# Moving one turn, three row loads, four bit copies and two late products in a fused hash-attention and SwiGLU kernel

## The chip, the core and the metric

The kernel runs on one core of a Trainium2 chip. A core has five engines with a queue each: TensorE (PE, matrix products; its weight loads are shown as PEld), VectorE (DVE), ScalarE (ACT), GpSimd (POOL) and SyncE (SP, which here only starts DMAs). Each engine takes its instructions strictly in the order of its queue; an instruction that waits holds up all behind it. The metric is device time of one execution in microseconds (us), the smaller the better.

## The reference

Attention in which a query sees only the keys of its own hash bucket, and then a gated feed-forward layer on the result:

```python
q_bits = (einsum('bhsd,dk->bhsk', q, proj) > 0)      # 6 bits for each token
k_bits = (einsum('bhsd,dk->bhsk', k, proj) > 0)
mask   = q_bucket[..., :, None] == k_bucket[..., None, :]
scores = where(mask, q @ k.T / sqrt(64), -1e9)
attn   = softmax(scores)                             # denominator + 1e-9
x      = (attn @ v), heads side by side              # 3072 x 512
xn     = x / sqrt(mean(x*x) + 1e-6) * rms_g
out    = (silu(xn @ w_gate) * (xn @ w_val)) @ w_out
```

q, k and v are (4, 8, 768, 64) in float32, proj is 64 x 6, w_gate and w_val are 512 x 1536, w_out is 1536 x 512; out is 3072 x 512 in float32.

## The kernel before

**Tiles.** The mask costs no product of its own: beside the 64 rows of a head, the operands of the score product (the tiles QK, six buffers that rotate) carry 12 rows of hash bits, scaled so that a pair of tokens of different buckets gets a score that exp takes to nothing. So the contraction runs over 76 rows (`KROWS`), or over 128 where the buffer's rows 64 to 127 were cleared with zeros once (`clear_rows`, line 138; `score_rows`, line 141).

Work goes by half units: a pair of key tiles of one head, for one half `w` of a batch (384 tokens, eight halves in all). `SLOTS` lists them, 6 for each pair of heads, in the order of `TURNS`: half 0 with head pair 0, half 1 with pair 0, half 0 with pairs 1, 2 and 3, half 1 with pairs 1, 2, 3, then batch 1 likewise. Pair 2 of half 0 is half units 18 to 23. In each half unit PE makes the scores (`scores`, lines 350 to 358, into s_ps, two buffers), ACT the exponentials (`probs`, line 365, into psb), and some half units later PE the product with v (`av`, line 377, into o_ps, of which there is one buffer). After two heads DVE takes o_ps out (`attn_out`, otmp of line 392, rcp of line 397); then x is otmp times rcp and sq is x squared (`attn_x`, lines 404 and 416, on POOL, or on DVE for pairs 2 and 3 of half 0), and DVE sums sq over the columns (`sumsq`, line 420). When all four pairs of a half are summed, the norm (lines 427 to 433), the scaling and the turning of x follow, and the feed-forward layer of that half is spread over the half units that come after (lines 473 to 503).

**Inputs.** Rows of q, k and v come by DMA from SP's queue into nine raw buffers (`load_rows`, line 113; 384 KB for a pair of heads). A new load waits until the old content of its buffer has been used. PE turns the rows (`turn_pe`, t_ps of line 181), DVE copies the result to kT and qT (`keep`, line 189), POOL and some ACT copies cast it into QK (`cast_half`, lines 195 and 197). The hash is a product of kT, qT and proj on PE (line 221, d_ps) and a comparison on DVE (`signs`, line 228); the bits are then copied into the rows of QK by DVE (lines 261 and 281) or by small DMAs on SP (lines 259 and 279). For pair 2 the hash is made at half unit 12; its first four bit blocks are copied by DVE, the other four by SP, and scores 19 are the first to need one of SP's.

**The order.** It is written out by hand: `at(s, f, ...)` puts a step into half unit `s` of `plan`, with a rank, and the loop at the end issues for each half unit the scores of the next one, the steps of rank below 3, the exponentials, and then the other steps by rank:

```python
for s in range(NS + 48):
    if 1 < s + 1 < NS:
        scores(s + 1)
    todo = steps(s)
    n = sum(r < 3 for r, _, _ in todo) if s < NS - 1 else 0
    for _, _, f in todo[:n]:
        f()
    if s < NS - 1:
        probs(s + 1)
    for _, _, f in todo[n:]:
        f()
```

What one half unit issues on an engine stands behind all that earlier ones issued there. The weights of the feed-forward layer (wg, wv, wo) are loaded by DMAs that POOL starts (lines 549 and 555); a load in POOL's queue stands behind the casts and products issued before it.

`idle` (line 345) makes products of ones with ones whose result nobody reads; eight stand ahead of scores 0 and six ahead of scores 3.

Of the kernel before, what the change touches and what calls it, by code (L numbers as in the profile page):

```python
# [8 lines left out]
FP32 = mybir.dt.float32  # L9
# [7 lines left out]
S = 768  # L17
# [31 lines left out]
def kernel(  # L49
# [34 lines left out]
    pq = const.tile([128, 48], FP32, name="pq")  # L84
    thr = const.tile([128, 1], FP32, name="thr")
    scl = const.tile([128, 1], FP32, name="scl")
    mhalf = const.tile([128, 3], FP32, name="mhalf")
# [49 lines left out]

    def clear_rows(i):
        nc.gpsimd.memset(qkbuf[i][D:128].rearrange("p h n -> p (h n)").bitcast(FP32), 0.0)

    def score_rows(b, hp):
        return slice(0, 128 if (b, hp) in ((1, 0), (1, 1)) or b > 1 else KROWS)

# [206 lines left out]
    def scores(g):  # L350
        w, h, p = SLOTS[g]
        ps = scps.tile([128, 2, 512], FP32, name="s_ps")
        idle(ps[:, 0, HALF:512], {0: 8, 3: 6}.get(g, 0))
        for j in range(2):
            nc.tensor.matmul(  # L355
                ps[:, j, 0:HALF], k_cols(w // 2, h, 2 * p + j), q_cols(w, h),
                start=True, stop=True,
            )
        sps[g] = ps
# [25 lines left out]
    def attn_out(w, hp):  # L385
        b = w // 2
        if w not in x:
            x[w] = xpool.tile([128, 3, DMODEL], FP32, name="x")
            ssp[w] = xpool.tile([128, 3, 4], FP32, name="ssp")
        o = ot.pop((w, hp))  # L390
        tmp = spool.tile([128, 3, 2, 66], FP32, name="otmp")
        nc.vector.tensor_add(  # L392
            tmp[:, :, :, 0:65], o[:, :, :, 0:65],
            cvb[b % 2][:, 2 * hp : 2 * hp + 2, 0:65].unsqueeze(1).to_broadcast([128, 3, 2, 65]),
        )
        r = spool.tile([128, 3, 2, 1], FP32, name="rcp")
        nc.vector.reciprocal(r, tmp[:, :, :, 64:65])  # L397
        return tmp, r

    def attn_x(w, hp, tmp, r):  # L400
        xd = x[w][:, :, 128 * hp : 128 * hp + 128]
        urgent = (w, hp) in ((0, 2), (0, 3))
        eng = nc.vector if urgent else nc.gpsimd
        eng.tensor_mul(  # L404
            xd.rearrange("p c (h d) -> p c h d", h=2), tmp[:, :, :, 0:64],
            r.to_broadcast([128, 3, 2, 64]),
        )
        sq = spool.tile([128, 3, 128], FP32, name="sq")
        if urgent:
            for c in range(3):  # L410
                nc.vector.scalar_tensor_tensor(
                    out=sq[:, c], in0=xd[:, c], scalar=1.0, in1=xd[:, c],
                    op0=ALU.mult, op1=ALU.mult, accum_out=ssp[w][:, c, hp : hp + 1],
                )
        else:
            nc.gpsimd.tensor_mul(sq, xd, xd)  # L416
        return sq
# [98 lines left out]

    nc.vector.memset(ones16, 1.0)
    make_identity(nc, ident)
    nc.gpsimd.dma_start(out=pn[64:128], in_=proj)
# [22 lines left out]
    for i in range(2):  # L542
        nc.gpsimd.memset(vls[i][:, :, :, 64:65], 1.0)
        nc.gpsimd.memset(vsum[i][:, :, 64:65], 6.0)
    clear_rows(4)
    clear_rows(5)

# [36 lines left out]
    cast_half(0, 0, "q", 0, nc.scalar)  # L584
    columns_of_proj()
    idle(wz[:, 0:128], 5)
    bits0 = hash_head(0)
# [37 lines left out]
    for h in range(2):  # L625
        at(1 + h, cast_half, 0, h, "q", 1)
        at(h, (bits0, bits1)[h], (nc.vector,), 3)

    for hp, turns, sv in ((1, (1, 2, 3, 5), 8), (2, (7, 8, 9, 10), 17), (3, (12, 13, 14, 15), 22)):
        for i, s in enumerate(turns):  # L630
            at(s, keep_pair, 0, hp, i)
            at(s + 1, casts, 0, hp, i)
            if i % 2:
                at(s + 2, cast_half, 0, 2 * hp + i // 2, "q", 0, nc.scalar)
        at(sv, v_prep, 0, hp)

    for h, s in ((2, 4), (3, 7)):
        at(s, hash_one, h)
        for t in range(3):
            at(s + 1 + t, lambda h=h, t=t: moves[h]((nc.vector,), t), rank=5)  # L640
    for hp, s, slots in ((2, 12, (13, 14, 15, 16)), (3, 17, (18, 19, 20, 21))):
        at(s, hash_pair, 0, hp)
# [4 lines left out]
    for i, (t, src) in enumerate(((wg, moe_w_gate), (wv, moe_w_val))):  # L647
        at(2 + 4 * i, load_w, t, src, 0, 768)
        at(19 + 5 * i, load_w, t, src, 768, 1536)
        at(38 + 7 * i, load_wo, 6 * i, 6 * i + 6)  # L650
# [4 lines left out]
    for hp, loads, turns, sh, evens, sv in (  # L655
        (0, (9, 11, 13), (20, 21, 24, 27), 33, (41, 42), (27, 44)),
        (1, (13, 14, 36), (29, 31, 33, 35), 40, (45, 47), (49, 51)),
    ):
# [42 lines left out]

    for i, s in ((2, 76), (3, 78), (0, 97), (1, 98)):
        at(s, clear_rows, i, rank=6)
# [22 lines left out]
    for w in range(8):  # L726
        for h in range(H):
# [85 lines left out]
```

## Time and profile before

| what | value |
|---|---|
| median of three runs | 329.41 us (329.21 to 329.52) |
| the profiled execution | 329.47 us |
| its span on the core | 327.6 us |
| PE busy | 321.5 us, 98% |
| DVE, ACT, POOL busy | 72%, 64%, 50% |
| granted PE clock | 0.998 |

In the rows of a timeline the first number is the start in us from the span's start, the second the time until the end of the last of the merged instructions; then come engine, line, operation, output and input, their shapes, and how many instructions are merged. In brackets stands the idle time of the engine just before, and what ended it. A row of windows gives the stretch, its length, the busy time of PE, PEld, DVE, ACT and POOL with the number of instructions, the granted clock, the DMA engines' mean share, and GB/s. In a row of the chain stand start, length, and what the time went to.

### The profile page before, as it was taken

To read this page: it belongs to the slowest core of one execution; us is meant where nothing else is said; L and a number is where in the kernel's file an instruction comes from. 1 tells how busy PE (TensorE), PEld (TensorE's weight loads), DVE (VectorE), ACT (ScalarE), POOL (GpSimd) and SP (SyncE) were. 2 spreads that over 40 slices of the span, in tenths; PEclk is the share of its full clock that TensorE was granted. 3 is DMA by queue.
4 is the path that set the end of the run, shared out by engine and by line. 5 is a ranking of instruction groups with operands and counts; after the bars stand their busy time and mean duration, and the time that the engine had idled before them with its cause. 6 is when DMAs were issued, how large, how long until landed. Compare 5 with 4: busy or idle time off the path is not lost.

```text
span 327.6 us, 7853 instructions
## 1 busy us (share of the span) xinstructions
PE 321.5 (98%) x2975; PEld 199.5 (61%) x2975; DVE 234.9 (72%) x526; ACT 208.1 (64%) x324; POOL 165.4 (50%) x238
## 2 busy tenths in 40 slices
PE   8998999999999999999999999999999999999995
PEld 7576766655566556655566656566566656655654
DVE  4798896888598976989487865967267824793860
ACT  3788986775576666657576766667677766423331
POOL 7887977278658685686734274733221320230000
PEclk9999999999999999999999999999999999999999
DMA  7998988984359729911470814001200012002002
GB/s 216 358 212 244 165 131 154 151 179 70 119 109 172 128 48 226 155 39 26 130 128 18 150 24 152 3 18 22 78 32 2 11 24 98 0 3 96 2 0 97
DMA packets 85509, 32.69 MB, mean 100 GB/s; under 512 B 70376, under 2 KB 82400, under 8 KB 85472
## 3 DMA queue, kind: packets, MB, share of 16 engines
q1 hardware_dynamic: 81392, 27.28, 35.2%
q0 software_dynamic: 3712, 4.72, 9.3%
q8 instruction: 23, 0.38, 0.5%
q10 hardware_dynamic: 368, 0.20, 0.2%
q14 instruction: 14, 0.11, 0.1%
HBM read 28.58 MB, written 6.29 MB: 106 GB/s over the span
## 4 chain that ended last, share of the span: by engine, by line
PE 94%; DMA 2%; ACT 2%; DVE 0%; issue 0%; DVEq 0%; ACTq 0%
PE v_ps L483 19%; PE s_ps L355 19%; PE y_ps L496 18%; PE g_ps L473 15%; PE o_ps L377 10%; PE d_ps L221 4%; PE s_ps L473 4%; PE t_ps L181 2%; DMA QK<-bits 2%; ACT psb L365 1%; PE z_ps L348 1%; PE x_ps L458 1%; DMA out_dram<-ysb 1%; PE m_ps L336 1%; DVE bits L228 0%
## 5 line engine op out<-in xcount | busy, mean ns | idle before, releaser
L365 ACT ACTIVATE psb<-s_ps 128x768 f16<-128x768 f32 x192 | 150.7, 809 | 30.1 <-PE s_ps L355 28.1
L355 PE MATMUL s_ps<-QK 128*128 128x384 f16 (+1 forms) x384 | 93.7, 326 | 1.3 <-DMA QK<-bits 0.5
L483 PE MATMUL v_ps<-xnT,wv 128*128 128x384 f16 x384 | 78.1, 326 | 0.0
L496 PE MATMUL y_ps<-wo,ht 128*128 128x512 f16 x276 | 69.2, 379 | 0.0
L404 POOL TENSOR_TENSOR x<-otmp,rcp 128x384 f32<-128x384 f32 x30 | 25.7, 857 | 83.4 <-DVE rcp L397 83.2
L377 PEld LDWEIGHTS <-psb 128*128 128x128 f16 x1152 | 51.7, 98 | 21.8 <-issue 3.7
L475 ACT ACTIVATE t<-g_ps 128x384 f32<-128x384 f32 x78 | 38.2, 490 | 40.7 <-PE g_ps L473 38.2
L473 PE MATMUL g_ps<-xnT,wg 128*128 128x384 f16 x312 | 63.5, 326 | 0.0
L484 DVE SCALAR_TENSOR_TENSOR t<-t,g_ps 128x384 f32<-128x384 f32 x78 | 42.9, 550 | 28.3 <-ACT t L475 28.2
L485 DVE SCALAR_TENSOR_TENSOR ht<-t,v_ps 128x384 f16<-128x384 f32 x96 | 53.2, 554 | 11.5 <-PE v_ps L483 1.0
L377 PE MATMUL o_ps<-vl,psb 128*128 128x65 f16 x1152 | 56.0, 193 | 0.0
L483 PEld LDWEIGHTS <-wv 128*128 128x128 f16 x384 | 36.5, 98 | 22.9
L473 PEld LDWEIGHTS <-wg 128*128 128x128 f16 x384 | 36.1, 98 | 23.0
L496 PEld LDWEIGHTS <-ht 128*128 128x128 f16 x276 | 26.3, 98 | 26.5 <-issue 2.1
L355 PEld LDWEIGHTS <-QK 128*128 128x128 f16 (+1 forms) x384 | 31.1, 97 | 16.8 <-issue 3.1
L503 ACT COPY ysb<-y_ps 128x512 f32<-128x512 f32 x23 | 13.5, 585 | 24.3 <-PE y_ps L496 23.7
L392 DVE TENSOR_TENSOR otmp<-o_ps,cvb 128x390 f32<-128x390 f32 x32 | 17.9, 559 | 14.9 <-PE o_ps L377 14.8
L416 POOL TENSOR_TENSOR sq<-x 128x384 f32<-128x384 f32 x30 | 25.5, 849 | 2.4
L213 POOL CAST QK<-kT 64x768 f16<-64x768 f32 x20 | 17.0, 848 | 10.8 <-DVE kT L205 8.9
L213 POOL CAST QK<-qT 64x768 f16<-64x768 f32 x20 | 16.5, 823 | 10.8 <-DVE qT L205 8.1
L205 DVE STREAM_TRANSPOSE kT<-kL 128x192 f32<-128x192 f32 x40 | 19.7, 521 | 0.0
L205 DVE STREAM_TRANSPOSE qT<-qL 128x192 f32<-128x192 f32 x40 | 19.4, 518 | 0.0
(81 smaller groups left out, 307.2 us busy)
## 6 DMA issues: line engine op xcount, KB each, us to landing
vL<-in_v_dram SPq DMA_DIRECT2D x16, 384.0 KB
out_dram<-ysb SPq DMA_DIRECT2D x23, 256.0 KB
kL<-in_k_dram SPq DMA_DIRECT2D x40, 96.0 KB
qL<-in_q_dram SPq DMA_DIRECT2D x40, 96.0 KB
kL<-in_k_dram SPq DMA_DIRECT2D x5, 384.0 KB
qL<-in_q_dram SPq DMA_DIRECT2D x5, 384.0 KB
wg<-in_moe_w_gate_dram POOLq DMA_DIRECT2D x2, 768.0 KB, 8.5
wv<-in_moe_w_val_dram POOLq DMA_DIRECT2D x2, 768.0 KB, 9.6
```

The costliest lines, as they stand in the source:

```text
L205: nc.vector.transpose(dst.rearrange("p (c t r) -> p r c t", c=6, r=4)[:, r : r + 1], src.rearrange("p (r c) d -> p r c d", r=4)[:, r : r + 1],
L213: nc.gpsimd.tensor_copy(QK[b, hp][0:64, hh, o : o + S], T0[b, hp, which][64 * hh : 64 * hh + 64, :])
L355: nc.tensor.matmul(ps[:, j, 0:HALF], k_cols(w // 2, h, 2 * p + j), q_cols(w, h), start=True, stop=True,)
L365: nc.scalar.activation(psb[w, h][:, p], sps.pop(g)[:, :, 0:HALF], AF.Exp, scale=ESCALE,)
L377: nc.tensor.matmul(o[:, c, hh, 0:65], psb[w, h][:, jt // 2, jt % 2, 128 * c : 128 * c + 128], vls[b % 2][:, h, v_chunk(b, h, jt), 0:65], s ...
L404: eng.tensor_mul(xd.rearrange("p c (h d) -> p c h d", h=2), tmp[:, :, :, 0:64], r.to_broadcast([128, 3, 2, 64]),)
L473: nc.tensor.matmul(g, wg[:, kt, fs], xnT[w][:, kt], start=(kt == 0), stop=(kt == 3))
L475: nc.scalar.activation(t, g, AF.Tanh, scale=0.5)
L483: nc.tensor.matmul(vv, wv[:, kt, fs], xnT[w][:, kt], start=(kt == 0), stop=(kt == 3))
L484: nc.vector.scalar_tensor_tensor(out=t, in0=t, scalar=1.0, in1=g, op0=ALU.add, op1=ALU.mult)
L485: nc.vector.scalar_tensor_tensor(out=ht[w][:, ft], in0=t, scalar=0.5, in1=vv, op0=ALU.mult, op1=ALU.mult)
L496: nc.tensor.matmul(y, ht[w][:, ft, c * 128 : (c + 1) * 128], wo[:, ft, :], start=(ft == 0), stop=(ft == NF - 1),)
```

## The change

- Scores 3 lose their six idle products. In the same place of PE's order stands the turn of q of head 2 (pair 1), which was one half unit later.
- The copies of the last bit block of heads 0 and 1 on DVE move from half units 0 and 1 to 2 and 4, to the end of each.
- The second bit copy of pair 2 on DVE moves from half unit 14 to 13.
- x and sq of pair 0 move to half units 22 (half 0; was 8) and 24 (half 1; was 17), and their sums to 24 and 26, ahead of the otmp of pair 2. The sum of pair 1 of half 0 moves from 24 to 22. otmp and rcp get a third buffer, sq has one instead of two.
- The row loads of batch 1 for pair 0 (k, q, v) move from half units 9, 11 and 13 to 3, 3 and 9, those of pair 1 (k, q) from 13 and 14 to 9. In SP's queue k and q of pair 0 now stand ahead of the bits of heads 2 and 3, and v, k, q ahead of those of pair 2.
- The second half of wg is loaded at half unit 21 instead of 19, that of wv at 25 instead of 24.
- Buffers 1, 2, 4 and 5 are cleared at the start, by POOL, POOL, ACT and DVE (in two parts), where it was 4 and 5 by POOL; buffer 0 follows at half unit 50 and 3 at 78, where it was 2, 3, 0 and 1 at 76 to 98. All scores but those of pairs 0 and 3 of batch 0 contract over 128 rows.

On POOL this gives the following order around half units 17 to 26, as the two kernels list it: v of pair 2; x, sq of pair 1; wg; two casts of kT; v of pair 3; a cast of qT; x, sq of pair 0 for half 0; x, sq of pair 0 for half 1; wv. On DVE the three sums stand one behind another, but for one copy of kT, just ahead of the otmp of pair 2.

```diff
-    def clear_rows(i):
-        nc.gpsimd.memset(qkbuf[i][D:128].rearrange("p h n -> p (h n)").bitcast(FP32), 0.0)
+    def clear_rows(i, eng=nc.gpsimd, heads=(0, 1)):
+        for h in (heads if eng is nc.vector else (0,)):
+            part = qkbuf[i][D:128, h] if eng is nc.vector else (
+                qkbuf[i][D:128].rearrange("p h n -> p (h n)"))
+            part = part.bitcast(FP32)
+            if eng is nc.scalar:
+                eng.copy(part, zcol[D:128].to_broadcast([D, 2 * S]))
+            else:
+                eng.memset(part, 0.0)
 
     def score_rows(b, hp):
-        return slice(0, 128 if (b, hp) in ((1, 0), (1, 1)) or b > 1 else KROWS)
+        return slice(0, KROWS if (b, hp) in ((0, 0), (0, 3)) else 128)
...
-        idle(ps[:, 0, HALF:512], {0: 8, 3: 6}.get(g, 0))
+        idle(ps[:, 0, HALF:512], {0: 8}.get(g, 0))
...
-        tmp = spool.tile([128, 3, 2, 66], FP32, name="otmp")
+        tmp = spool.tile([128, 3, 2, 66], FP32, name="otmp", bufs=3)
...
-        r = spool.tile([128, 3, 2, 1], FP32, name="rcp")
+        r = spool.tile([128, 3, 2, 1], FP32, name="rcp", bufs=3)
...
-        sq = spool.tile([128, 3, 128], FP32, name="sq")
+        sq = spool.tile([128, 3, 128], FP32, name="sq", bufs=1)
...
-    clear_rows(4)
-    clear_rows(5)
+    clear_rows(1)
+    clear_rows(2)
+    clear_rows(4, nc.scalar)
+    clear_rows(5, nc.vector, (0,))
...
     columns_of_proj()
+    clear_rows(5, nc.vector, (1,))
...
-        at(h, (bits0, bits1)[h], (nc.vector,), 3)
-
-    for hp, turns, sv in ((1, (1, 2, 3, 5), 8), (2, (7, 8, 9, 10), 17), (3, (12, 13, 14, 15), 22)):
+        at(2 + 2 * h, (bits0, bits1)[h], (nc.vector,), 3, rank=6)
+
+    for hp, turns, sv in ((1, (1, 1, 3, 5), 8), (2, (7, 8, 9, 10), 17), (3, (12, 13, 14, 15), 22)):
...
-    for hp, s, slots in ((2, 12, (13, 14, 15, 16)), (3, 17, (18, 19, 20, 21))):
+    for hp, s, slots in ((2, 12, (13, 13, 15, 16)), (3, 17, (18, 19, 20, 21))):
...
-        at(19 + 5 * i, load_w, t, src, 768, 1536)
+        at(21 + 4 * i, load_w, t, src, 768, 1536)
...
-        (0, (9, 11, 13), (20, 21, 24, 27), 33, (41, 42), (27, 44)),
-        (1, (13, 14, 36), (29, 31, 33, 35), 40, (45, 47), (49, 51)),
+        (0, (3, 3, 9), (20, 21, 24, 27), 33, (41, 42), (27, 44)),
+        (1, (9, 9, 36), (29, 31, 33, 35), 40, (45, 47), (49, 51)),
...
-    for i, s in ((2, 76), (3, 78), (0, 97), (1, 98)):
+    for i, s in ((0, 50), (3, 78)):
...
-                if (w, h) == (1, 1):
+                if w < 2 and h == 1:
                     at(end, o_first, w, 0, rank=4.5)
-                    at(end + 3, o_last, w, 0, rank=4.5)
+                    at(22 + 2 * w, o_last, w, 0, rank=4.5)
+                    at(24 + 2 * w, s_step, w, 0, rank=4)
                 else:
                     at(end, o_step, w, h // 2, rank=4.5)
-                if (w, h) not in ((0, 5), (0, 7)):
+                if (w, h) not in ((0, 1), (0, 5), (0, 7), (1, 1)):
                     late = 3 if h == 7 and w < 7 else 4
-                    at(end + late, s_step, w, h // 2, rank=5)
+                    if (w, h) == (0, 3):
+                        at(22, s_step, w, 1, rank=4)
+                    else:
+                        at(end + late, s_step, w, h // 2, rank=5)
```

More of the change, by code (lines that the diff above doesn't have):

```diff
@@ L85 @@
     thr = const.tile([128, 1], FP32, name="thr")
+    zcol = const.tile([128, 1], FP32, name="zcol")
     scl = const.tile([128, 1], FP32, name="scl")
@@ L517 @@
     nc.vector.memset(ones16, 1.0)
+    nc.vector.memset(zcol, 0.0)
     make_identity(nc, ident)
```

## The prediction

> **What bounds the kernel now.** I read the page first, then the windows, then the chain of waits, then each engine's timeline between 8 and 46 us.
>
> ```profile
> span 327.6 us, 7853 instructions
> PE 321.5 (98%) x2975; PEld 199.5 (61%) x2975; DVE 234.9 (72%) x526; ACT 208.1 (64%) x324; POOL 165.4 (50%) x238
> ...
> 20.00:30.00 10.00, 9.13 (x117) 6.03 (x116) 8.85 (x21) 8.51 (x15) 8.93 (x15) 1.00 0.93 228
> ...
> 50.00:60.00 10.00, 10.00 (x94) 6.46 (x92) 7.56 (x16) 7.72 (x14) 6.20 (x10) 1.00 0.91 152
> ...
> 22.78 0.68 DVE bits L228
> ...
> 23.48 5.21 DMA QK<-bits
> ...
> 28.83 0.34 PE s_ps L355
> ...
> 29.19 0.82 ACT psb L365
> ```
>
> PE is the bound. From 50 us its windows are full, so whatever time is won or lost ahead of that is carried to the end one for one. The loss lies in the attention-only start: 20 to 30 us lacks 0.87 us of PE, and the chain passes there from the hash bits of pair 2 through a DMA of 5.21 us to the scores. Every edit but the later clears falls in this start; I price each as a shift of PE at about 46 us, and carry it to the end.
>
> **The clears.** Two POOL clears stay where they were (other buffers). One more is a scalar copy of 1536 columns ahead of the first qT copy; DVE gets two of 768 columns, one ahead of its first kT copy, one ahead of the first signs.
>
> ```profile
> 5.54 0.48 ACT L189 COPY qT<-t_ps 128x384 f32<-128x384 f32 x1 [2.94 <-PE t_ps L181]
> ...
> 4.90 0.56 DVE L189 COPY kT<-t_ps 128x384 f32<-128x384 f32 x1 [1.40 <-PE t_ps L181]
> ...
> 6.98 0.68 DVE L228 TENSOR_SCALAR bits<-d_ps,thr,scl 128x384 f16<-128x384 f32 x1 [1.34 <-PE d_ps L221]
> ```
>
> Four copies of 384 columns are 1.92 us, inside ACT's idle 2.94. For a DVE clear the nearest row is a copy of 384 columns, 0.56, so 768 columns cost 1.12 at most, inside 1.40 and 1.34. These idle times are the cover; without it up to 1.1 us would stand ahead of the first hash, and below nothing it can't go, since nothing is taken away there. I take 0. The later clears are POOL's, three become one in the PE-full part: 0. Contraction over 128 rows instead of 76 leaves the product its 384 columns: 0.
>
> **The turn in the place of idle products, and two bit moves put back.**
>
> ```profile
> 10.97 0.50 PE L348 MATMUL s_ps<-ones 128*128 128x128 f16 x6 [0.24 <-ACT psb L365]
> 11.30 0.49 PE L355 MATMUL s_ps<-QK 76*128 76x384 f16 x2
> ...
> 10.54 0.50 POOL L261 COPY QK<-bits 12x384 f16<-12x384 f16 x1 [0.83 <-DVE bits L228]
> ```
>
> The six products hold PE from 10.97 to 11.30, 0.33 us. The turn of q fills the wait ahead of them instead, and vanishes from behind these scores. But the scores wait for POOL's bits, done at 11.04, and the next ones for ACT, so not all of 0.33 is gained there; DVE's two copies for pair 1 come earlier too, which shortens the next hash. I take 0.4 us by 21 us, bounds 0.1 and 0.7.
>
> **Two bits of pair 2 moved in one half unit.**
>
> ```profile
> 26.09 0.25 DVE L281 COPY QK<-bits 12x384 f16<-12x384 f16 x1
> ...
> 26.49 0.48 PE L355 MATMUL s_ps<-QK 76*128 76x384 f16 x2 [0.15 <-DVE QK L281]
> ```
>
> The second move ends at 26.34, and scores 18 start right behind it. Moved ahead of a turn copy and o_ps, and with one reduction gone from DVE, it frees PE some 0.3 us. Both gains bring PE earlier to scores 19, where it waits for the DMA of the bits. They count only if that DMA comes earlier as well.
>
> **Row loads ahead of pair 2's bits.** All go through SP's one queue.
>
> ```profile
> 19.26 0.46 SPq L117 DMA_DIRECT2D kL<-in_k_dram  x1
> ...
> 23.48 3.53 SPq L279 DMA_DIRECT2D QK<-bits  x4
> ...
> vL<-in_v_dram SPq DMA_DIRECT2D x16, 384.0 KB
> ...
> 12.00:15.50 3.50, 3.50 (x42) 2.13 (x40) 2.63 (x7) 3.00 (x5) 3.32 (x7) 1.00 1.07 377
> 15.50:19.50 4.00, 4.00 (x50) 2.84 (x49) 3.69 (x9) 3.17 (x6) 3.84 (x7) 1.00 1.14 195
> 19.50:22.50 3.00, 3.00 (x39) 1.98 (x36) 2.78 (x8) 3.00 (x6) 2.22 (x4) 1.00 1.16 208
> 22.50:26.50 4.00, 3.85 (x55) 3.15 (x52) 3.80 (x10) 3.52 (x7) 3.71 (x9) 1.00 1.09 280
> 26.50:28.00 1.50, 1.50 (x18) 0.56 (x19) 1.37 (x5) 1.40 (x3) 1.21 (x3) 1.00 0.28 90
> 28.00:32.50 4.50, 3.73 (x54) 2.88 (x51) 3.50 (x8) 3.53 (x6) 2.85 (x4) 1.00 0.92 276
> ```
>
> The last two columns are the DMA engines' share and GB/s. The engines are full from 12 to 26.5 us. Before, two row loads (k and q of batch 1, pair 0, from 19.26) stood ahead of the bits; the other three (v of that pair, k and q of pair 1) followed them in SP's queue. Now all five are issued first: two at half unit 3, three at 9. They wait for raw buffers: the last one needs pair 2's q turned at half unit 10, which PE does before the hash at 12, so the issue itself isn't late. But 3 x 384 KB more are ahead of the bits in engines that have no free time. At 377 GB/s that is 3.1 us, at the 276 of the window in which they run now, 4.3. The lull of 26.5 to 28 can take in at most 0.72 of 1.5 us, 1.1. So the bits land at 28.69 + 3.1 - 1.1 = 30.7 to 28.69 + 4.3 = 33.0. If the bits needn't stand behind the rows, they land 5.21 us after an issue some 0.4 earlier, 0.4 us before now. I take +2.5 (31.2), nearest to the row loads at full rate with half the lull used; ends -0.4 and +4.3. Queued behind the waiting loads on SP are also the bits of heads 2 and 3, read first at half unit 30: 0. The second half of wg, two half units later and behind x on POOL, is read first at half unit 50: 0.
>
> ACT passes such a delay on:
>
> ```profile
> 29.19 3.82 ACT L365 ACTIVATE psb<-s_ps 128x768 f16<-128x768 f32 x5 [0.91 <-PE s_ps L355]
> 33.17 6.92 ACT L365 ACTIVATE psb<-s_ps 128x768 f16<-128x768 f32 x9 [0.15 <-PE s_ps L355]
> ```
>
> From 29.19 to 40.09 it is at work but for 0.15 us, so what starts later at 29.19 ends later.
>
> **x and squares of pair 0 later: the largest term.** POOL's queue, DVE's and PE's, as they are now:
>
> ```profile
> 30.13 0.81 POOL L549 DMA_DIRECT2D wg<-in_moe_w_gate_dram  x1
> 32.53 0.89 POOL L404 TENSOR_TENSOR x<-otmp,rcp 128x384 f32<-128x384 f32 x1 [1.60 <-DVE rcp L397]
> 33.50 0.82 POOL L416 TENSOR_TENSOR sq<-x 128x384 f32<-128x384 f32 x1
> 34.27 1.05 POOL L197 CAST QK<-kT 64x384 f16<-64x384 f32 x2
> 35.39 0.82 POOL L321 CAST vl<-vL 128x768 f16<-128x768 f32 x1
> 36.28 0.50 POOL L197 CAST QK<-qT 64x384 f16<-64x384 f32 x1
> ...
> 31.66 0.56 DVE L392 TENSOR_TENSOR otmp<-o_ps,cvb 128x390 f32<-128x390 f32 x1
> ...
> 34.63 0.55 DVE L420 TENSOR_REDUCE ssp<-sq 128x3 f32<-128x384 f32 x1
> 35.53 0.56 DVE L392 TENSOR_TENSOR otmp<-o_ps,cvb 128x390 f32<-128x390 f32 x1 [0.35 <-PE o_ps L377]
> ...
> 30.70 0.44 PE L377 MATMUL o_ps<-vl,psb 128*128 128x65 f16 x9
> ...
> 36.50 0.44 PE L377 MATMUL o_ps<-vl,psb 128*128 128x65 f16 x9
> ```
>
> The row of 32.53 is x of pair 1, half 0; it waits for rcp, which hangs on PE's o_ps of 30.70. In the new order POOL does, from there, in a row: x, sq of that pair; wg's issue; two kT casts; v; a qT cast; then x, sq of (0,0) and x, sq of (1,0), which used to be done ahead of all these. POOL can't start them in its idle time ahead of 32.53, as they are queued behind it.
>
> DVE then has, ahead of the otmp of 35.53, the reductions of both of these sq. So otmp waits for POOL. By starts, on the clock of before: rcp some 0.18 earlier, since a move and a reduction are gone ahead of it, x at 32.35; sq at 33.32 (+0.97); wg at 34.09 (+0.77); kT at 34.95 (issue 0.81 and a step); v at 36.07 (+1.12); qT at 36.96 (+0.89); x(0,0) at 37.45; its sq at 38.4, done at 39.2. With one sq buffer the second sq waits for DVE's reduction of the first (0.55): 40.15 to 40.97. The second reduction ends at 41.6, otmp runs 41.65 to 42.2. The one o_ps buffer is then free, and PE's o_ps of 36.50 starts at 42.25: 5.75 us late. ACT has no backlog then, so PE may win back a little: I take +5.6. Shortest: the same chain at the busy times alone, without steps between, has otmp end at 41.8, +5.3. Longest: DVE, which is 6.1 late itself, sets the time, 6.1. Nothing gains here: the idle POOL ahead of 32.53 is on no one's path.
>
> **Sum.** The profiled execution took 329.47 us (median of the runs 329.41, so 0.06 above). 329.47 + 2.5 (bits) + 5.6 (DVE behind POOL) = 337.6; the 0.4 and 0.3 of the start end in the wait for the bits.
>
> [...] Half rate of TensorE stands at the start of this trace:
>
> ```profile
> 1.05 3.17 PE L348 MATMUL z_ps<-ones 128*128 128x128 f16 x28 [1.05 <-DVE pm L520]
> ...
> 7.56 0.61 PE L348 MATMUL s_ps<-ones 128*128 128x128 f16 x8
> ```
>
> The first 28 products come every 107 ns or so, the later 8 every 56. If an idle PE falls back to that rate, the 5.7 us of idleness would bring it back, and the wait ahead of the bits, some 3 us, perhaps. The half rate lasted between 3.17 us (the 28) and 6.5 (1.05 to 7.56), so each fall costs 1.6 to 3.3 us; I take 2, near the end that is shown. No row of before has PE idle that long after the start, so nothing here tells.
> [...]
>
> **The rivals.**
> A, as summed: 336.3 to 338.8 (bits 1.5 to 3.7 later). Chance 0.42.
> B, POOL's delay, but the bits no later: 329.47 + 5.6 - 0.4 = 334.7. For it: small transfers may pass the rows; against: engines full to 26.5. 0.20.
> C, A and one fall to half rate: 339.6. 0.25.
> D, bits late, squares in time: 332.0. Against: POOL's order. 0.05.
> E, faster: POOL finishes both squares before DVE asks at 35.4. Then the start's 0.4 and 0.3 count, and of PE's 0.87 at 20 to 30 us some 0.5, if the bits land with them: 329.47 - 1.2 = 328.3. It decides where POOL is 5.6 us quicker than its rows. 0.05. Elsewhere 0.03.
>
> **How the numbers follow.** 337.6 is A. The range 333.8 to 340.8 holds B, A and most of C. A measurement here can tell 0.2% (0.7 us). Slower is A to D and 0.02 of the rest: 0.94; the same 0.01; faster 0.05.
>
> **What would show it.** A DVE reduction that waits some 4 us for POOL's sq, PE's o_ps waiting behind otmp, bits that land over 7 us after their issue, and no six products near 11 us. Wrong if DVE's reductions near 35 us wait under 1 us, or PE is full from 30 to 45 us.

## The result and the profile after

The changed kernel takes 340.67 us (median of 5 runs, 340.2 to 341.17); the kernel before took 329.49 us beside it (329.21 to 330.88). The ratio is 1.0331, with a 95% interval of 1.0309 to 1.0353: 11.2 us slower. The forecast was 337.6 us, 8.1 us slower, with 333.8 to 340.8 as its range. The result is in the range, but only 0.1 us below its upper end.

The head of the page of the changed kernel, the busy times (its part 1) and the row of the granted clock from part 2 (40 slices of the span, in tenths of the full rate):

```profile
span 338.9 us, 7840 instructions
...
PE 325.6 (96%) x2969; PEld 201.8 (60%) x2969; DVE 236.1 (70%) x529; ACT 210.0 (62%) x325; POOL 163.7 (48%) x236
...
PEclk9997859999999999999999999999999999999999
```

Span and time grew by 11.3 and 11.2 us. PE is busy for 4.1 us more with six instructions fewer: its products took longer. The row of the clock says where: in the slices from 25 to 51 us TensorE had less than full rate. The mean granted clock is 0.980 instead of 0.998.

The windows of the changed kernel, with the bounds used for the one before where these apply:

```profile
26.50:28.00 1.50, 1.50 (x20) 0.51 (x18) 1.28 (x5) 1.50 (x3) 1.25 (x2) 1.00 1.07 298
28.00:32.50 4.50, 0.94 (x4) 0.43 (x4) 0.81 (x3) 0.41 (x2) 0.18 (x1) 0.72 0.33 107
32.50:36.50 4.00, 4.00 (x31) 3.14 (x30) 1.65 (x5) 2.77 (x4) 0.39 (x1) 0.50 0.62 98
36.50:41.50 5.00, 4.95 (x62) 3.46 (x60) 2.13 (x5) 4.35 (x7) 4.64 (x8) 0.97 0.91 123
41.50:46.00 4.50, 0.14 (x3) 0.15 (x4) 1.74 (x4) 0.84 (x2) 4.34 (x6) 0.74 0.74 132
46.00:52.00 6.00, 6.00 (x62) 4.50 (x60) 4.30 (x13) 2.75 (x4) 3.26 (x6) 0.63 0.85 129
```

There are two holes in PE, 28 to 32.5 and 41.5 to 46 us, and a stretch at half rate lies over the end of each and behind it (the clock is the third number from the end: 0.72 in 28:32.5 and 0.50 in 32.5:36.5, 0.74 in 41.5:46 and 0.63 in 46:52). The lull in which the DMA engines had a share of 0.28 before, 26.5 to 28, is now full, 1.07.

What ends the holes stands in PE's timeline:

```profile
31.64 1.12 PE L363 MATMUL s_ps<-QK 128*128 128x384 f16 x3 [3.56 <-DMA QK<-bits]
...
33.06 0.83 PE L363 MATMUL s_ps<-QK 128*128 128x384 f16 x2
...
37.40 0.49 PE L363 MATMUL s_ps<-QK 76*128 76x384 f16 x2
...
45.85 0.68 PE L385 MATMUL o_ps<-vl,psb 128*128 128x65 f16 x9 [4.38 <-DVE otmp L400]
46.34 0.83 PE L363 MATMUL s_ps<-QK 128*128 128x384 f16 x2
```

The first hole ends with the bits of pair 2, the second with DVE's otmp. A pair of score products takes 0.83 us behind each hole and 0.49 at full rate, so the half rate makes the products longer and is not only a number of the clock.

For the first hole, the step of the chain of waits that leads to it:

```profile
23.54 7.96 DMA QK<-bits
```

Before, the same DMA took 5.21 us from 23.48. For the second, DVE's and then POOL's timeline:

```profile
43.08 0.55 DVE L428 TENSOR_REDUCE ssp<-sq 128x3 f32<-128x384 f32 x1 [3.67 <-POOL sq L424]
44.77 0.56 DVE L428 TENSOR_REDUCE ssp<-sq 128x3 f32<-128x384 f32 x1 [1.14 <-POOL sq L424]
45.24 0.55 DVE L400 TENSOR_TENSOR otmp<-o_ps,cvb 128x390 f32<-128x390 f32 x1
```

```profile
36.11 0.89 POOL L412 TENSOR_TENSOR x<-otmp,rcp 128x384 f32<-128x384 f32 x1 [7.92 <-DVE rcp L405]
...
41.32 0.82 POOL L412 TENSOR_TENSOR x<-otmp,rcp 128x384 f32<-128x384 f32 x1
42.23 0.82 POOL L424 TENSOR_TENSOR sq<-x 128x384 f32<-128x384 f32 x1
43.01 0.82 POOL L412 TENSOR_TENSOR x<-otmp,rcp 128x384 f32<-128x384 f32 x1
43.91 0.83 POOL L424 TENSOR_TENSOR sq<-x 128x384 f32<-128x384 f32 x1
```

The two moved x and sq run at 41.32 to 44.74, behind the work that starts at 36.11; POOL stood idle for 7.92 us before it. DVE's sums wait for them, 3.67 and 1.14 us, and otmp, which needs neither, stands behind the sums.

The account. Scores are numbered by half unit; the table gives the start of the second product of some of them, counted from that of scores 0, so that the start of a run, which varies by up to 0.9 us, is left out. The last column is the end of the span less the time of scores 44.

| kernel | scores 10 | 18 | 19 | 30 | 44 | from 44 to the end |
|---|---|---|---|---|---|---|
| before | 10.37 | 18.12 | 20.30 | 28.50 | 41.65 | 277.44 |
| after | 9.95 | 17.91 | 23.12 | 38.13 | 53.08 | 277.28 |
| after less before | -0.42 | -0.21 | +2.82 | +9.63 | +11.43 | -0.16 |

Up to scores 18 the changed kernel is ahead. At scores 19 it is 2.8 us behind, between 19 and 30 it loses 6.8 more (the half rate, then the wait for otmp), between 30 and 44 another 1.8 (half rate), and behind that nothing.

### The profile page after: what moved, and what is told of

It is laid out like the page before. It is cut to its first block, busy times and chain, and to the rows that moved or that the text cites. A ratio compares the mean times of both kernels' runs of the same rounds, so it can differ in the third digit from the quotient of the medians.

```text
span 338.9 us, 7840 instructions
## 1 busy us (share of the span) xinstructions
PE 325.6 (96%) x2969; PEld 201.8 (60%) x2969; DVE 236.1 (70%) x529; ACT 210.0 (62%) x325; POOL 163.7 (48%) x236
## 4 chain that ended last, share of the span: by engine, by line
PE 89%; DMA 3%; DVE 2%; POOL 2%; ACT 2%; issue 1%; DVEq 0%; POOLq 0%; ACTq 0%
PE v_ps L491 18%; PE y_ps L504 18%; PE s_ps L363 17%; PE g_ps L481 15%; PE o_ps L385 9%; PE d_ps L229 4%; PE s_ps L481 3%; DMA QK<-bits 2%; PE t_ps L189 1%; ACT psb L373 1%; PE z_ps L356 1%; PE x_ps L466 1%; POOL sq L424 1%; POOL x L412 1%; DMA out_dram<-ysb 1%
## 5 line engine op out<-in xcount | busy, mean ns | idle before, releaser
L363 PE MATMUL s_ps<-QK 128*128 128x384 f16 (+1 forms) x384 | 96.0, 333 | 4.1 <-DMA QK<-bits 3.6
L385 PEld LDWEIGHTS <-psb 128*128 128x128 f16 x1152 | 53.0, 99 | 27.2 <-DVE otmp L400 4.8
L385 PE MATMUL o_ps<-vl,psb 128*128 128x65 f16 x1152 | 57.3, 195 | 4.5 <-DVE otmp L400 4.4
L491 PEld LDWEIGHTS <-wv 128*128 128x128 f16 x384 | 36.5, 98 | 22.8
L428 DVE TENSOR_REDUCE ssp<-sq 128x3 f32<-128x384 f32 x30 | 16.0, 533 | 5.2 <-POOL sq L424 5.2
```

What stands on the lines that cost most here:

```text
L363: nc.tensor.matmul(ps[:, j, 0:HALF], k_cols(w // 2, h, 2 * p + j), q_cols(w, h), start=True, stop=True,)
L385: nc.tensor.matmul(o[:, c, hh, 0:65], psb[w, h][:, jt // 2, jt % 2, 128 * c : 128 * c + 128], vls[b % 2][:, h, v_chunk(b, h, jt), 0:65], s ...
L491: nc.tensor.matmul(vv, wv[:, kt, fs], xnT[w][:, kt], start=(kt == 0), stop=(kt == 3))
```

## The experiments

The theory: late bits and DVE's queue behind POOL's late squares are two causes, each costs on its own, and on top of each wait comes a fall of the clock. The rivals were that one of them alone is at work and the other hangs on it, that the half rate is hidden behind other engines, and that it is POOL's lateness as such, not DVE's order, that costs. All runs start from the changed kernel unless said otherwise. The kernel before took 329.38 to 329.47 us beside them.

| run | edit | us, median (range) | ratio to before, 95% |
|---|---|---|---|
| e3_both_back | squares and loads as before | 329.66 (329.24 to 330.34) | 0.9985 to 1.0014 |
| e1_squares_back | squares as before, loads early | 333.74 (332.63 to 334.11) | 1.0076 to 1.0142 |
| e11_bits_warm | the same, PE kept at work in the wait | 333.06 (332.84 to 333.27) | 1.0079 to 1.0133 |
| e8_loads_back_wg21 | loads as before, squares late | 336.07 (335.55 to 337.32) | 1.0190 to 1.0223 |
| e10_squares_warm | the same, PE kept at work in the wait | 335.31 (334.32 to 335.87) | 1.0147 to 1.0212 |
| e2_loads_back | loads and wg as before, squares late | 336.07 (335.0 to 337.26) | 1.0147 to 1.0224 |
| e4_warm | all as changed, PE kept at work in both waits | 337.91 (337.57 to 338.36) | 1.0202 to 1.0275 |
| e5_sums_late | sums behind otmp | 336.2 (335.35 to 337.04) | 1.0179 to 1.0214 |
| e6_three_back | squares and three loads as before | 330.2 (330.02 to 331.04) | 1.0016 to 1.0038 |
| e7_wv_behind | e6, wv later, bit copy at 14 | 330.63 (329.78 to 333.73) | 1.0022 to 1.0074 |
| e9_three_back_wg19 | e6, wg at 19, bit copy at 14 | 329.49 (329.08 to 330.26) | 0.9985 to 1.0013 |
| e12_sum_behind | e9, one sum behind otmp | 328.62 (328.23 to 329.31) | 0.9962 to 0.9985 |

**The bits alone.** x, sq and sums as before the change (the main lines; otmp and rcp have their old number of buffers again, too):

```diff
-        sq = spool.tile([128, 3, 128], FP32, name="sq", bufs=1)
+        sq = spool.tile([128, 3, 128], FP32, name="sq")
...
-                if w < 2 and h == 1:
+                if (w, h) == (1, 1):
                     at(end, o_first, w, 0, rank=4.5)
-                    at(22 + 2 * w, o_last, w, 0, rank=4.5)
-                    at(24 + 2 * w, s_step, w, 0, rank=4)
+                    at(end + 3, o_last, w, 0, rank=4.5)
...
```

> The changed kernel with x, squares and sums of pair 0 at their half units of before (and the buffers of before); everything else as changed. The theory (two waits, late bits and DVE behind POOL, each with a fall of TensorE to half rate behind it) takes out the wait for POOL and its fall: PE's rows of before and after differ by 2.8 us at scores 19 and by 4.8 at scores 24, so 329.5 + 4.8 = 334.3 us. If the half rate has another cause than idleness, it costs 329.5 + 2.8 = 332.3 or stays above 336. If only the squares made it slower, and the late bits are hidden, 329.5.

Measured: 333.74 us, 4.3 over before. Its PE timeline and its windows:

```profile
32.09 1.12 PE L363 MATMUL s_ps<-QK 128*128 128x384 f16 x3 [3.70 <-DMA QK<-bits]
```

```profile
28.00:32.50 4.50, 0.80 (x11) 0.40 (x8) 2.15 (x4) 0.36 (x1) 2.09 (x3) 0.88 0.36 116
32.50:36.50 4.00, 4.00 (x42) 3.10 (x41) 1.39 (x4) 3.20 (x5) 0.02 (x1) 0.71 0.51 81
```

The wait for the bits is there without the late squares, and with it half rate (0.71 in 32.5:36.5). How much of the 4.3 us is the clock, a second run tells, in which products nobody reads keep PE at work in the wait:

```diff
-        idle(ps[:, 0, HALF:512], {0: 8}.get(g, 0))
+        idle(ps[:, 0, HALF:512], {0: 8, 19: 60}.get(g, 0))
```

> The early row loads alone (squares as before), with 60 idle products ahead of scores 19, so that PE doesn't stand still while the bits come; without these products it took 333.74 us. Theory: PE still resumes when the bits land, but at full rate, and of the 4.3 us some 1.2 go (the stretch from scores 19 to 30 was that much longer than in the kernel before): 332.5 us (332.0 to 333.0). Rival: PE's half rate is hidden behind ACT and DVE there, then 333.7.

Measured: 333.06 us. The same windows, and two steps of its chain of waits:

```profile
28.00:32.50 4.50, 4.50 (x82) 4.24 (x81) 2.21 (x4) 0.93 (x3) 2.19 (x3) 1.00 0.35 113
32.50:36.50 4.00, 3.70 (x55) 3.06 (x52) 2.56 (x7) 3.79 (x6) 1.21 (x2) 1.00 0.56 88
```

```profile
28.33 3.35 PE s_ps L356 x60
31.68 0.34 PE s_ps L363 x2
```

PE is at work all through 28 to 32.5 us, and the clock stays at 1.00. By the medians the bits alone cost 333.06 - 329.38 = 3.7 us, and the fall of the clock behind them 0.7, less than the 1.2 expected. Both are bounds: in this execution the chain goes from the 60 products straight to scores 19, so these products, and not the bits, ended the wait, and the bits may have been there earlier. So the bits cost at most 3.7 us and the fall at least 0.7. The bounds needn't be far off: scores 19 come here at 23.22 from scores 0, and at 23.12 to 23.74 in the other runs with all five loads early. But as the fastest of the four runs without these products, 332.63, is below all four with them, the sizes are rough. That there is a price shows in the stretch from scores 19 to 30: at half rate it took 9.37 us, at full rate 8.52, before 8.20.

**The squares alone.** Row loads as before; wg's second half stays at half unit 21:

```diff
-        (0, (3, 3, 9), (20, 21, 24, 27), 33, (41, 42), (27, 44)),
-        (1, (9, 9, 36), (29, 31, 33, 35), 40, (45, 47), (49, 51)),
+        (0, (9, 11, 13), (20, 21, 24, 27), 33, (41, 42), (27, 44)),
+        (1, (13, 14, 36), (29, 31, 33, 35), 40, (45, 47), (49, 51)),
```

> Row loads at the half units of the kernel before, squares and sums late as in the changed kernel, and wg's second half at half unit 21 as there: the squares' part alone, without the weight load that got ahead of pair 3's bits in the earlier run. Theory: no wait for bits over 0.5 us; DVE waits near 4 us for POOL's sq ahead of otmp, PE some 4.5 us behind o_ps, and one fall of the clock behind it, of which some 1.5 us stay: 329.5 + 4.5 + 1.5 = 335.5 us (334.5 to 336.5). Rival: the loss at DVE's queue comes only from being added to late bits; then under 333.

Measured: 336.07 us, 6.6 over before. DVE's and PE's timelines:

```profile
39.67 0.55 DVE L428 TENSOR_REDUCE ssp<-sq 128x3 f32<-128x384 f32 x1 [4.07 <-POOL sq L424]
41.36 0.55 DVE L428 TENSOR_REDUCE ssp<-sq 128x3 f32<-128x384 f32 x1 [1.14 <-POOL sq L424]
41.83 0.55 DVE L400 TENSOR_TENSOR otmp<-o_ps,cvb 128x390 f32<-128x390 f32 x1
```

```profile
42.44 0.68 PE L385 MATMUL o_ps<-vl,psb 128*128 128x65 f16 x9 [5.47 <-DVE otmp L400]
```

With the bits nearly in time (a wait of 1.01 us at scores 19), otmp starts at 41.83 and o_ps at 42.44: the chain on POOL and DVE that the prediction added up, step by step, to 41.65 and 42.25. From the start of x of pair 1 to otmp it took 9.08 us, where the prediction had 9.30. The loss doesn't need late bits. Again with PE kept at work:

```diff
-        idle(ps[:, 0, HALF:512], {0: 8}.get(g, 0))
+        idle(ps[:, 0, HALF:512], {0: 8, 29: 70}.get(g, 0))
```

> The late squares and sums alone (row loads as before, wg at half unit 21), with 70 idle products ahead of scores 29, so that PE doesn't stand still while DVE waits for POOL; the run without these products took 336.07 us. Theory: the wait itself stays (otmp near 41.8 us), but the clock stays at full rate, and the time falls by 1 to 2 us, to 334.1 to 335.1; that is the price of the late squares by themselves, 4.6 to 5.7 us. Rival: the half rate costs nothing there, since PE has time in hand behind the wait: 336 us as without.

Measured: 335.31 us, a little slower than expected; the profiled execution, at 334.32, is the fastest of the four. The clock stays at 1.00 and otmp still comes late (40.69 us; in that execution scores 19 came 0.8 us earlier). Behind the 70 products PE still waits 1.56 us for otmp, so here the products didn't end the wait. So the squares cost 335.31 - 329.38 = 5.9 us at full rate, and the clock 0.8 on top. That difference is small beside the spread of both runs, 1.8 and 1.6 us, so its size is rough.

**A run that hit its number another way.** Loads and wg as before:

```diff
-        at(21 + 4 * i, load_w, t, src, 768, 1536)
+        at(19 + 5 * i, load_w, t, src, 768, 1536)
-        (0, (3, 3, 9), (20, 21, 24, 27), 33, (41, 42), (27, 44)),
-        (1, (9, 9, 36), (29, 31, 33, 35), 40, (45, 47), (49, 51)),
+        (0, (9, 11, 13), (20, 21, 24, 27), 33, (41, 42), (27, 44)),
+        (1, (13, 14, 36), (29, 31, 33, 35), 40, (45, 47), (49, 51)),
```

> The changed kernel with the row loads and the second half of wg at their half units of before; squares late as changed. The theory: no wait of 3.6 us for the bits, one wait for POOL remains, shorter by wg's issue of 0.8 us, which is ahead of x again: 5.6 - 0.8 + 2.1 for one fall to half rate - 0.5 for the early edits = 335.9 us. Without the fall 333.8. If only the loads made it slower, under 329.5.

Measured: 336.07 us, as expected, but PE's timeline shows another sequence; POOL's row of wg is beside it:

```profile
36.13 0.34 PE L363 MATMUL s_ps<-QK 76*128 76x384 f16 x1 [2.39 <-DMA QK<-bits]
...
42.35 0.45 PE L385 MATMUL o_ps<-vl,psb 128*128 128x65 f16 x9 [1.74 <-DVE otmp L400]
```

```profile
28.23 0.78 POOL L560 DMA_DIRECT2D wg<-in_moe_w_gate_dram  x1
```

With x and sq gone from ahead of it, POOL issues wg's 768 KB at 28.23 instead of 30.13, just ahead of SP's bits of pair 3, and these come 2.4 us late for PE. The wait for otmp is correspondingly shorter. That is why wg stands at 21 in the run above; the edit of wg in the change, priced at nothing, has a purpose there.

**Both waits at full rate.** The changed kernel with products in both waits:

```diff
-        idle(ps[:, 0, HALF:512], {0: 8}.get(g, 0))
+        idle(ps[:, 0, HALF:512], {0: 8, 19: 60, 29: 70}.get(g, 0))
```

> The changed kernel with 60 products of ones ahead of scores 19 and 70 ahead of scores 29, which nobody reads: at 56 ns each they take 3.4 and 3.9 us inside PE's two waits. The theory that idleness brings the half rate: the rate stays full, both waits stay, and 2.0 + 2.1 us go: 336.6 us. If the half rate comes with something else (a load of the DMA engines, a fixed time), 340.7 or more, and the granted clock still shows half behind the waits.

Measured: 337.91 us, slower than expected. Its window behind the first wait and PE's row behind the second:

```profile
32.50:36.50 4.00, 3.70 (x59) 3.08 (x56) 2.32 (x6) 3.80 (x6) 0.93 (x2) 1.00 0.41 66
```

```profile
45.17 0.45 PE L385 MATMUL o_ps<-vl,psb 128*128 128x65 f16 x9 [1.56 <-DVE otmp L400]
```

No half rate is left (1.00 where the changed kernel has 0.50), and o_ps still starts at 45.17 instead of 45.85. So the two falls together cost 340.67 - 337.91 = 2.8 us. The expectation had 4.1, the excess of the stretches that ran at half rate; a part of that was hidden: o_ps came only 0.68 us earlier, since POOL's chain, which ends the second wait, goes at its own pace once it has begun. Here the 60 and 70 products did not end the waits: PE still waited 0.64 us for the bits behind the first, and 1.56 for otmp. Without the clock the change costs 337.91 - 329.44 = 8.5 us; the parts by themselves, at most 3.7 and some 5.9, make up to 9.6, so up to 1.1 us of one wait lies beside the other.

**DVE's order or POOL's lateness.** POOL as late as in the changed kernel, DVE's sums behind the otmp's, a buffer for each of the two squares:

```diff
-                    at(24 + 2 * w, s_step, w, 0, rank=4)
+                    at(29 + 3 * w, s_step, w, 0, rank=6)
...
-        sq = spool.tile([128, 3, 128], FP32, name="sq", bufs=1)
+        if w < 2 and hp == 0:
+            sq = spool.tile([128, HALF], FP32, name="t", bufs=3)
+            sq = sq.rearrange("p (c d) -> p c d", c=3)
+        else:
+            sq = spool.tile([128, 3, 128], FP32, name="sq", bufs=1)
```

> Everything as in the changed kernel (x and squares of pair 0 just as late on POOL), but DVE's two sums of them stand behind the otmp's of pair 2 and pair 3 (half units 29 and 32 in the place of 24 and 26), and these two squares get a buffer each. Theory: the second loss of the changed kernel is DVE's queue, in which otmp stands behind sums that wait for POOL. Then DVE no longer waits near 38 to 44 us, o_ps of pair 2 comes free on time, only the wait for the bits is left, and the time is that of the run with the squares put back, 333.7 us (333 to 334.5). Rival: POOL's lateness itself is what costs (its casts and the work behind them, or the norm that needs the sums): then PE is late again at 41 to 46 us and the time stays above 336.5.

Measured: 336.2 us, between the two. Rows of DVE, of POOL and of PE:

```profile
39.23 0.56 DVE L400 TENSOR_TENSOR otmp<-o_ps,cvb 128x390 f32<-128x390 f32 x1 [0.86 <-PE o_ps L385]
...
43.04 0.54 DVE L432 TENSOR_REDUCE ssp<-t 128x3 f32<-128x384 f32 x1
```

```profile
49.41 0.89 POOL L445 TENSOR_TENSOR rstd<-ms,mhalf 128x3 f32<-128x3 f32 x1
```

```profile
51.21 0.40 PE L470 MATMUL x_ps<-ident,xn 128*128 128x128 f16 x4 [2.40 <-DVE xn L456]
```

otmp now waits for PE, as it should, and the hole at 41 to 46 us is gone: DVE's order made it. What is late now is the norm of half 0. The moved sum that it needs is there in time (43.04), but its rstd stands on POOL behind the late work: the chain of waits stays on POOL from 38 to 50 us, rstd starts at 49.41 (47.56 in the run with the squares in time and the bits as late), and PE waits 2.40 us for the scaled x, again with half rate behind it. The wait moves on to the next result of POOL that PE needs. Both theories held in part: in the changed kernel it is DVE's order that costs, and POOL's lateness would cost without it.

**The small edits at the start.** Squares and loads (wg and wv too) both as before; what stays is the early turn, the bit copies, the clears and the 128 rows:

```diff
-        (0, (3, 3, 9), (20, 21, 24, 27), 33, (41, 42), (27, 44)),
-        (1, (9, 9, 36), (29, 31, 33, 35), 40, (45, 47), (49, 51)),
+        (0, (9, 11, 13), (20, 21, 24, 27), 33, (41, 42), (27, 44)),
+        (1, (13, 14, 36), (29, 31, 33, 35), 40, (45, 47), (49, 51)),
...
-                if w < 2 and h == 1:
+                if (w, h) == (1, 1):
```

> Both taken back: the turn in the place of six idle products, the bit copies, the clears and the 128 rows alone. The theory: none of the loss remains, and the early gain of 0.4 to 0.7 us shows only if the bits of pair 2 land earlier; their landing hangs on DMA engines that are full, so 329.2 us, between 328.7 and 329.5. If the clears or the 128 rows cost something, over 329.7.

Measured: 329.66 us, no difference. Two rows of its PE timeline:

```profile
26.05 0.43 PE L385 MATMUL o_ps<-vl,psb 128*128 128x65 f16 x9 [0.56 <-DVE otmp L400]
...
28.74 0.65 PE L363 MATMUL s_ps<-QK 128*128 128x384 f16 x3 [0.61 <-DMA QK<-bits]
```

Scores 10 come 0.42 us earlier, counted from scores 0 (9.95 against 10.37); which of the small edits gives that, these runs don't separate. At scores 14, well ahead of the wait for the bits, 0.09 of it is left (14.22 against 14.31). At scores 18 the kernel is behind (18.39 against 18.12): with both bit copies of pair 2 in half unit 13, DVE's otmp of (1, 0) comes later, and PE waits 0.56 us for it; then it waits for the bits as before.

**Which loads delay the bits.** Squares as before, three of the five row loads behind the bits again:

```diff
-        (0, (3, 3, 9), (20, 21, 24, 27), 33, (41, 42), (27, 44)),
-        (1, (9, 9, 36), (29, 31, 33, 35), 40, (45, 47), (49, 51)),
+        (0, (3, 3, 13), (20, 21, 24, 27), 33, (41, 42), (27, 44)),
+        (1, (13, 14, 36), (29, 31, 33, 35), 40, (45, 47), (49, 51)),
```

> Squares and sums as before the change, and of the five row loads the three that stood ahead of pair 2's bits (v of pair 0, k and q of pair 1) put behind them again; k and q of pair 0 stay at half unit 3, and wg's second half at 21. Theory: these three loads are the whole delay of the bits, so the bits land near 28.7 us as in the kernel before, PE doesn't wait over 0.5 us at scores 19, and the time is 329.3 us (328.8 to 329.8). Rival: bits for the rows already queued (k and q of pair 0, now ahead of the bits of heads 2 and 3 as well) are enough to make them late, then part of the 4.2 us of the run with only the squares put back stays, over 331.

Measured: 330.2 us, 0.8 more than before, but not for the bits: scores 19 come at 19.88 from scores 0, 0.42 earlier than before. The three loads are the whole delay; k and q of pair 0, issued at 12 to 15 us, do no harm. The loss comes behind that:

```profile
36.98 0.43 PE L385 MATMUL o_ps<-vl,psb 128*128 128x65 f16 x9 [0.46 <-POOL vl L329]
```

With wg's issue (0.80 us on POOL) at half unit 21, it now stands ahead of the v cast for which PE waits here. Another 0.40 us goes to a wait for an otmp at 32.18.

**Towards a faster version.** First, from the run just shown, with 768 KB less in the DMA engines ahead of the bits and the second bit copy at half unit 14 again:

```diff
-        at(2 + 4 * i, load_w, t, src, 0, 768)
+        at(2 + 16 * i, load_w, t, src, 0, 768)
...
-    for hp, s, slots in ((2, 12, (13, 13, 15, 16)), (3, 17, (18, 19, 20, 21))):
+    for hp, s, slots in ((2, 12, (13, 14, 15, 16)), (3, 17, (18, 19, 20, 21))):
```

> A version meant to be faster than both: squares as before, the three row loads behind pair 2's bits, the second bit copy of pair 2 back at half unit 14, and the first half of wv loaded at half unit 18 in the place of 6, so that 768 KB less are in the DMA engines between 12 and 28 us. Theory: the bits wait for the bytes ahead of them, so with 768 KB less they land 2 to 3 us after their issue, near 26 us, PE has no wait at scores 19, and the 0.4 us of the early turn and the 0.4 of that wait count: 328.6 us (328.2 to 329.0). Rival: the load at 18 only moves the crowd on to pair 3's bits, read at scores 25 (near 33 us), as wg's load did: then 330 to 332; or the o_ps that waits for otmp takes the gain, then 329.4.

Measured: 330.63 us. The window shows that the engines are in fact free while the bits move:

```profile
22.50:26.50 4.00, 3.90 (x51) 3.11 (x50) 3.80 (x10) 3.42 (x7) 3.71 (x9) 1.00 0.07 14
```

Scores 19 come at 19.36 from scores 0, 0.94 earlier than before, and that is lost by scores 44 (41.92 against 41.65), by waits for otmp (0.44 us) and for the v cast (0.47 us). From there to the end another 0.69 us goes (278.13 against 277.44), with a wait of 0.55 us for bits at 84 us. So wv went back, and wg with it to half unit 19:

```diff
-        at(21 + 4 * i, load_w, t, src, 768, 1536)
+        at(19 + 5 * i, load_w, t, src, 768, 1536)
```

> A version meant to be faster than both: the early turn, the clears and the early k and q loads of pair 0 stay; squares as before, the three row loads behind pair 2's bits, the second bit copy of pair 2 back at half unit 14, and wg and wv as before the change (half units 19 and 24). In the run with three loads put back, scores 19 came 0.4 us earlier than in the kernel before when both are counted from scores 0 (19.88 against 20.30 us), and the loss came behind it: PE waited for POOL's v cast that stands behind wg. Theory: without that wait the stretch from scores 19 to 44 takes 21.35 us as before, and the time is 329.4 less 0.4 to 0.9, so 328.5 to 329.0. Rival: what is gained at scores 19 is lost at the next wait that ends on DVE or on ACT, then 329.3 to 329.7.

Measured: 329.49 us, the rival's number. DVE's and PE's rows of the wait that takes the gain:

```profile
30.15 0.56 DVE L428 TENSOR_REDUCE ssp<-sq 128x3 f32<-128x384 f32 x1 [0.82 <-POOL sq L424]
```

```profile
32.21 0.43 PE L385 MATMUL o_ps<-vl,psb 128*128 128x65 f16 x9 [0.45 <-DVE otmp L400]
```

It is the pattern of the large loss in small: a sum of pair 0 waits for POOL, and an otmp stands behind it. So the last edit:

```diff
-                    at(end + late, s_step, w, h // 2, rank=5)
+                    at(22 if (w, h) == (1, 1) else end + late, s_step, w, h // 2, rank=5)
```

> The run with three loads back, wg at half unit 19 and the second bit copy at 14 came out at 329.49 us: counted from scores 0 it was 0.70 us earlier than the kernel before at scores 19, but level with it at scores 29, because at 32.21 us PE waited 0.45 us for otmp of pair 1, which stood on DVE behind a sum (at 30.15) that waited for POOL's sq of pair 0, half 1. Here that sum goes to half unit 22, behind this otmp; nothing else differs. Theory: POOL's sq is what takes the gain, by way of DVE's queue, as in the changed kernel but smaller; without it scores 29 come 0.4 us earlier and the time is 329.0 us (328.8 to 329.2). Rival: ACT, at work almost without a break from 29 to 40 us, takes the gain instead, then 329.4 to 329.6.

Measured: 328.62 us, ratio 0.9974 (0.9962 to 0.9985), faster than the kernel before by 0.26%; the interval leaves out 1, but not by much. DVE's row of this otmp, and PE's next wait:

```profile
30.67 0.56 DVE L400 TENSOR_TENSOR otmp<-o_ps,cvb 128x390 f32<-128x390 f32 x1
```

```profile
32.97 0.34 PE L363 MATMUL s_ps<-QK 76*128 76x384 f16 x1 [0.36 <-DMA QK<-bits]
```

otmp starts at 30.67 instead of 31.59, PE's wait for it is gone, and the bits of pair 3 are late next. The mechanism is shown; the size is not explained in full. The median fell by 0.87 us, but scores 44 come only 0.21 earlier than without the edit (41.39 against 41.60); of the rest of the profiled executions' difference, 0.86 us, 0.27 lies ahead of scores 0 and 0.38 outside the span, where the edit does nothing.

## Why the prediction was right, and where its sizes were off

- **Its direction and its two mechanisms held.** Bits behind three more row loads, and DVE's sums waiting for POOL's squares ahead of otmp, were both there in the trace and each by itself in a run. The signs that it named were there: a sum that waits near 4 us (3.67), o_ps behind otmp, bits over 7 us after their issue (7.96), no six products near 11 us.
- **Late bits, +2.5.** They landed at 31.50 us (23.54 + 7.96) against the 31.2 forecast, 2.8 late. The sum had half of the lull used; all of it was used (share 1.07), which at the 377 GB/s taken would have left 2.0, so that rate was too high for this stretch. Alone and at full rate the early loads cost at most 3.7 us, of which 2.9 stand at scores 19.
- **DVE behind POOL, +5.6.** The chain summed from single rows gave otmp at 41.65, and the run with this part alone had it at 41.83. Its price is some 5.9 us alone. In the changed kernel PE comes to it later, so that its hole there is 4.38 us. One step was misread without effect: the second sq does not wait for DVE's reduction of the first, but follows its own x on POOL (43.01 and 43.91, while that reduction ended at 43.63).
- **The sum, 337.6, is where the prediction was off: it held no fall of the clock.** The changed kernel without half rate takes 337.91 us; its own 340.67 are that and 2.8 us of half rate. So the likeliest case, A (336.3 to 338.8), did not come; what came was its rival C, with a chance of 0.25 and one fall at 2 us. In place of one there were two, and they cost 2.8 together, not 2 each. That 340.67 still lies in the range, by 0.1 us, is luck: two falls at the 2 us each that the prediction took would have made 341.6. What made me keep the fall out of the likeliest case was that no row of before showed PE idle that long; but the trace before showed that half rate exists (products of ones every 107 ns at its start, every 56 ns later), and the two waits, of some 3 and 5.7 us, were forecast.
- **That 337.6 is so near 337.91 is in part luck, too.** The sum adds the two waits in full, 2.5 and 5.6. Measured one by one they are larger, at most 3.7 and some 5.9, and up to 1.1 us of them lies side by side, which the sum doesn't have; the two errors nearly cancel.
- **The rivals.** B (bits in time) falls with the run that has only early loads: 4.3 us. D (squares in time) falls with the sums' waits. E (faster) needed POOL to be 5.6 us quicker, and it took its rows' durations: 9.13 us from x of pair 1 to otmp (36.11 to 45.24), against the 9.30 summed.
- **The early turn, 0.4 by 21 us, was too much:** the lead is 0.42 us at scores 10, but 0.19 at scores 13 (near 21 us) and 0.08 at 14, well ahead of the wait for the bits. What takes it there was not followed up. **The second bit copy, 0.3, was wrong** where squares are in time: the copies in one half unit push otmp of (1, 0) back, and PE waits 0.56 us for that. In the changed kernel, with a sum gone from DVE, it is a gain of 0.1: the lead grows from 0.10 at scores 17 to 0.21 at 18. The step moved past otmp was not counted.
- **The clears at 0** held: ACT's zeros took 1.47 us ahead of its first qT copy, which starts at 5.54 as before. A score product took 326 ns over 128 rows and 325 ns over 76 in the trace before. From scores 44 on the changed kernel and ten of the runs, the squares late or not, take 277.27 to 277.32 us instead of 277.44 (the other two, with wv later and with products ahead of scores 19, take 278.13 and 277.70), so fewer clears and the rows count for at most 0.17 us, in their favour. **wg at 0** was right only in this combination: with the squares late and the loads as before, wg at its old place delays pair 3's bits; with the squares and the three loads as before, wg at its new place delays a v cast.

## What to carry to other kernels

When a step is moved behind other work on one engine, look for its readers on the other engines: what stands behind such a reader in its queue waits too, even if it needs nothing of the step (here otmp, behind sums that waited 3.67 and 1.14 us), and with one accumulator buffer that reached TensorE (4.38 us). Count with a fall of the clock at long waits of TensorE: here those of 2.39, 2.40, 3.56, 3.66, 3.70, 4.38 and 5.47 us each had one, one of 1.74 us had none. Find its share by keeping TensorE at work in the wait; the clock stayed at 1.00 in the three runs that did so. A wait removed is worth only the distance to the next: here an otmp, a cast and another otmp took the place of the bits one after the other, and a gain, 0.85 us by the medians, of which the trace shows 0.4 from scores 0 on, came only when all were out of the way.

## What the runs showed of the hardware

Stretches at half rate, added up from the granted clock of the windows, lasted 3.4 us (behind the wait for bits in the run with squares back; the run with loads and wg back; both of the run with the sums behind) or 6.8 us, twice that (both of the changed kernel, and the run with squares alone). Idle times of 3.56 and 4.38 us had it begin 1.9 and 2.2 us after PE stopped; but behind idle times of just 2.39 and 2.40 us it began 0.9 and 1.0 us after PE was at work again. Over all seven waits with a fall it began 1.9 to 4.1 us after PE stopped. In the run with loads and wg back PE waited another 1.74 us later on, at 40.61, and no fall followed. What sets the start and the two lengths is not shown.

The price of a fall was not its length times one half here. Some 3.4 us at half rate cost some 0.7 us by the medians (333.74 against 333.06, with ranges that overlap), and two stretches of 6.8 us cost 2.8. A part of each stretch lies in the wait itself: in the changed kernel 1.7 us of the first and 2.2 of the second. That the rest is hidden behind ACT, DVE and POOL fits the late start of o_ps in the run without half rate, but it was not measured by itself.

The bits came later with more queued ahead of them: the DMA of pair 2's bits took 5.21 us before, 7.96 behind 1152 KB more in SP's own queue. A load of 768 KB in POOL's queue, issued 0.6 us ahead of pair 3's bits on SP, went along with 2.39 us of waiting for these, although it is another queue; with that load issued at 34.49 the wait was gone. So a load in either queue went along with later bits here; how the DMA engines share their time between the two queues, none of the runs measures.
